# A recurrent-memory attention kernel whose streamed weights are loaded in halves, later, in a new order

## The chip, the cores and the metric

The kernel runs on one core of a Trainium2 chip. The metric is the device time of one execution in microseconds. Before the change three runs took 3192.28, 3196.55 and 3191.59 us (median 3192.28).

TensorE appears as PE for the matmuls and as PEld for the weight loads that overlap them; VectorE is DVE, ScalarE is ACT, GpSimd is POOL, and SyncE is SP, which here does nothing but issue DMAs.

## The reference

The input is 2048 tokens of width 640. It goes through two layers with the same weights; each layer has a part A and a part B, and each part is added to its input.

```python
# A: 64 segments of 32 tokens, one after the other, with a memory of 8 rows
for s in range(n_seg):
    h = concatenate([mem, x[s*32:(s+1)*32]])          # 40 rows of 640
    q, k, v = h @ Wq, h @ Wk, h @ Wv                  # 32 heads of 192
    p = softmax(where(mask, q @ k.T * 192**-0.5, -1e9))
    o = (p @ v) @ Wo                                  # 40 rows of 640
    mem = o[:8]; out[s] = o[8:]                       # the memory goes on
# B: on all tokens
h  = gelu(layernorm(x) @ w1)                          # 640 x 640
hs = shift_four_groups(h) @ w2                        # 640 x 640, by 1 or 2 tokens
x1 = x + hs
y  = x1 + gelu(layernorm(x1) @ w3) @ w4               # 640 x 1536 x 640
```

The memory makes part A sequential: segment s+1 needs the first 8 output rows of segment s. All of Wq, Wk, Wv (640 x 6144 each) and Wo are used in every segment.

## The kernel before, in words

The two layers run as two lanes, the second five segments behind the first, so that most of the 69 steps (`T_A`) work on one segment of each lane at once: 2 x 40 = 80 rows. A step of attention walks over four pairs of head groups (`NPAIR`; a group has 4 heads, so 768 columns of a weight, `GW`; a pair has 1536, `PW`). Odd steps walk the pairs backwards, so that the last pair of one step is the first of the next and its weights are kept. For each pair there are projections for keys and queries (L1743: the weight is the stationary operand, the 80 rows stream), values (L1790, L1817, L1848: the rows are stationary), and for each of its two groups scores (L1868), a softmax on DVE and ACT (L1880, L1887, L1891 to L1893), transposes (L1903), the product with the values (L1920) and the output projection (L1946). Between them lies part B of the segments that are through, in chunks of two steps (L2142 to L2476).

The weights do not all fit in SBUF. Of the five row blocks of 128 of a weight, a part stays in resident tiles (`wk`, `wq`, `wv`, `wo`, made once by `res_tile`), and `STREAM` says how many blocks of each pair are read again in every step: 4, 2, 2, 4 for keys and queries, 3, 1, 1, 4 for values. `load_pair` (L1587) streams each such block as one DMA of 128 rows x 1536 columns (384 KB) into a ring of 12 buffers (`RING_A`, tile name `wst`). One such block serves both groups of the pair, so its buffer comes free only after the second group's projections. Weights of part B go through a ring of 3 buffers (`load_b`, `wstB`). All of these DMAs stand in one queue, SP's, in order.

In which order each engine's instructions stand is decided ahead of time by `Plan.place`, which is a list scheduler with costs of its own: operations of an engine are sorted by a rank (the table `RANK`, else the due time), and placed when their operands are ready by its estimate. For SP it also waits until its estimate of the DMA backlog is under `DMA_AHEAD` us; such a DMA is called paced, and is given a wait on the matmul that should end just before it (`PACE`). In the first and last steps at most `FLYING` of SP's weight DMAs may be under way. SP's DMAs also take turns on eight completion semaphores, so that each waits until the eighth before it has landed. PE's order is fixed by this plan; the hardware then runs the queues as they stand, each waiting on semaphores.

For the last chunk of part B there is no step left that could cover its loads. `homes` lists places inside resident tiles of the last two pairs that are no longer needed; 13 of its 19 loads go there, and the other six into the streaming ring.

Of the kernel before, what the change touches and what calls it, by code (L numbers as in the profile page):

```python
# [11 lines left out]
bf16 = mybir.dt.bfloat16  # L12
# [10 lines left out]
RING_A = 12  # L23
# [33 lines left out]
DMA_ISSUE = 0.37  # L57
# [5 lines left out]
DMA_AHEAD = 1.0  # L63
DMA_AHEAD_ONE = 1.0
DMA_START = 375.0e3
RATE_ONE = 350.0e3
NSTEPS = 64
LAST_PACE = 0.55
FLYING = 5
# [9 lines left out]
        "apply_ln.f": (626742377, 1381540087, 2899948923, 3305595292,),  # L79
        "chunk.f1": (-45861084,),  # L80
        "chunk.f2": (-45659757,),
        "chunk.f3": (1142445880,),
        "chunk.fe": (681528837,),
        "chunk.fe3": (3558561887,),
        "chunk.fel": (929138305,),
        "chunk.fhr": (1690223076,),
        "chunk.fhs": (3263874326,),
        "chunk.fk0": (585175460,),
        "chunk.fk1": (2899747596,),
        "chunk.fs": (3237320380, 3237521706,),  # L90
        "chunk.ft": (256864035,),
        "chunk.ftl": (1386157383,),
        "chunk.fw": (1690089438, 1635248815, 1663407949, 3135586750, 2850300232, 2661990109, 3573417949,
            3572573150, 3675059769, 3969648649, 3957741830, 4039975132, 4549482156,),
        "chunk.fx": (257065362,),
        "chunk.fx0": (1526572645, 1386869158,),
        "chunk.fxu": (3348674608,),
        "gelu.f1": (1699890861, 1945196059, 3675261096, 3920708539, 4184197392, 4484921572, 4620347075,),
        "gelu.f2": (1699825810, 2028698272, 3681545875, 3947181960, 4202989764, 4549896008, 4584775502,),
        "gelu.f3": (1700027137, 2490379395, 3745281954, 3957725317, 4362469546, 4620334608, 4623504062,),  # L100
        "gelu.f4": (1944994732, 2631326347, 3850812073, 3948320419, 4362670872, 4550298661, 4623468787,),
        "ln_ops.f1": (429292543, 3237723033,),
        "ln_ops.f2": (585056509, 3305393966,),
        "load_b.fn": (-910488622, -944871371, -932829747, 2409305095, 2322445750, 2257234409, 2921458646,
            2661468021, 3186012878, 3602555507, 3601991726, 3600713583, 4110587825,),
        "transposes.f": (681327511, 3546956339,),
    },
    "chunk_0": {
        "apply_ln.f": (-9435854, 1110510770, 1460067902,),
        "chunk.f1": (-416043209635,),  # L110
        "chunk.f2": (-282216187950,),
        "chunk.f3": (166275964,),
        "chunk.fe": (-11203768,),
        "chunk.fe3": (1569789630,),
        "chunk.fel": (316814938,),
        "chunk.fhr": (608520262,),
        "chunk.fhs": (1149152527,),
        "chunk.fk0": (773149199,),
        "chunk.fs": (1129996849, 1129996849,),
        "chunk.ft": (-171210997,),  # L120
        "chunk.ftl": (166477291,),
        "chunk.fw": (574133776, 547786658, 574316317, 1085014019, 1105500739, 1129795522, 1570217486,
            1570328582, 1492728232, 3006190713, 3006190784, 3006714875, 3168347961,),
        "chunk.fx": (-84446892,),
        "chunk.fx0": (515277332, 361838522,),
        "chunk.fxu": (1578287371,),
# [8 lines left out]
        "transposes.f": (-54228973, 1485017325,),  # L135
    },
    "chunk_1": {
        "apply_ln.f": (56483562, 141981145, 1588087148, 1857952252,),
        "chunk.f1": (-5799992,),
        "chunk.f2": (69525817,),  # L140
        "chunk.f3": (141963611,),
# [1228 lines left out]
def kernel(  # L1370
# [16 lines left out]
    nc = tc.nc  # L1387
    P = 128
# [6 lines left out]
    KC = Dm // P  # L1395
# [1191 lines left out]
```

## Time and profile before

| what | value |
|---|---|
| median of three runs | 3192.28 us |
| the profiled execution, time | 3207.95 us |
| the profiled execution, span | 3206.2 us, 158605 instructions |
| PE busy | 3098.9 us, 97% |
| PEld, DVE, ACT, POOL busy | 86%, 64%, 54%, 16% |
| moved by DMA | 859.45 MB, mean 268 GB/s |
| SP's queue (q1) | 796.08 MB, 75.6% of the 16 engines' time |

PE's busy time says where PE had a matmul under way. What is left, some 107 us, are gaps, and each has something that ended it: a DMA that landed, a result of DVE or ACT, or "issue", where no semaphore was being waited for. The first 100 us hold the largest part of it, since nothing is in SBUF yet. The queue of DMAs is the second thing to look at: q1 carries the weights, q8 the instructions themselves in blocks of 16 KB, q0 the transfers that POOL issues.

### The profile page before, as it was taken

The numbers are of one execution on the slowest core, as the hardware profiler recorded it, in microseconds if no ns is written. First come the engines' busy times: TensorE is split into PE (matmuls) and PEld (weight loads), VectorE is DVE, ScalarE is ACT, GpSimd is POOL, SyncE is SP. The second block draws the span as 40 slices with busy tenths as digits, with TensorE's granted clock in tenths as the row PEclk, the third lists the DMA queues.
The fourth block names the chain that finished last, engine by engine and source line by source line (L and its number), as shares of the span: only waits on it lengthen the run. The fifth ranks groups of instructions, "written<-read, shape, count | busy, mean of one in ns | idle before, by whom it ended". The sixth has DMA issues, their size and how long they took to land.

```text
span 3206.2 us, 158605 instructions
## 1 busy us (share of the span) xinstructions
PE 3098.9 (97%) x70198; PEld 2765.0 (86%) x70201; DVE 2053.9 (64%) x6448; ACT 1720.1 (54%) x3985; POOL 497.6 (16%) x983
## 2 busy tenths in 40 slices
PE   5899999999999999999999999999999999999997
PEld 4778888988988989888889888888898889888876
DVE  3566566666666666666666666666666666666665
ACT  1335555555555555565555555555565565556443
POOL 1001111111111111111111111111111111110000
PEclk7999999999999999999999999999999999999999
DMA  9888788878888888888788888888888888888786
GB/s 378 275 262 260 252 281 267 259 247 275 267 263 266 288 256 266 261 279 268 252 274 278 257 258 261 276 257 260 289 264 256 260 276 269 260 267 284 256 283 213
DMA packets 421673, 859.45 MB, mean 268 GB/s; under 512 B 48334, under 2 KB 216223, under 8 KB 420984
## 3 DMA queue, kind: packets, MB, share of 16 engines
q1 hardware_dynamic: 396776, 796.08, 75.6%
q0 software_dynamic: 24032, 53.12, 5.5%
q8 instruction: 550, 9.01, 1.2%
q14 instruction: 139, 1.14, 0.1%
q10 hardware_dynamic: 176, 0.09, 0.0%
HBM read 823.73 MB, written 25.37 MB: 265 GB/s over the span
## 4 chain that ended last, share of the span: by engine, by line
PE 90%; DMA 6%; issue 2%; DVE 1%; ACT 1%; POOL 0%; SPq 0%; POOLq 0%; DVEq 0%; ACTq 0%
PE psk L1743 17%; PE psy L1946 17%; PE psq L1743 17%; PE psv L1790 12%; PE pso L1920 5%; PE pss L1868 4%; PE psv L1817 3%; PE y L2422 3%; PE psh L2376 3%; PE pst L1903 2%; PE psv L1848 2%; DMA wst<-in_A_Wq_dram 1%; PE hs L2313 1%; PE psh L2253 1%; DMA wst<-in_A_Wk_dram 1%
## 5 line engine op out<-in xcount | busy, mean ns | idle before, releaser
L1743 PEld LDWEIGHTS <-wst 128*128 128x128 bf16 x19872 | 826.7, 99 | 88.6 <-issue 39.4
L1946 PE MATMUL psy<-oT,wo 128*128 128x80 bf16 (+1 forms) x16560 | 712.1, 200 | 13.5 <-issue 7.0
L1946 PEld LDWEIGHTS <-wo 128*128 128x128 bf16 x16560 | 639.2, 99 | 54.9 <-issue 30.7
L1778 ACT CAST V<-psv 32x384 bf16<-32x384 f32 (+3 forms) x1032 | 487.5, 473 | 363.1 <-PE psv L1790 276.2
L1743 PE MATMUL psq<-hT,wst 128*128 128x80 bf16 (+1 forms) x9936 | 558.3, 200 | 10.8 <-DMA wst<-in_A_Wq_dram 7.0
L1743 PE MATMUL psk<-hT,wst 128*128 128x80 bf16 (+1 forms) x9936 | 543.3, 200 | 19.5 <-issue 7.8
L1753 ACT CAST qT<-psq 128x480 bf16<-128x480 f32 (+1 forms) x552 | 292.6, 530 | 348.6 <-PE psq L1743 277.1
L1880 DVE CUSTOM_DVE_ANT_1 pss<-pss,mask 80x320 f32<-80x320 f32 (+2 forms) x552 | 257.1, 466 | 296.8 <-ACT V L1778 145.4
L1768 DVE CAST kT<-psk 64x160 bf16<-64x160 f32 (+1 forms) x1104 | 339.6, 308 | 161.5 <-PE psk L1743 78.2
L1928 ACT CAST oT<-pso 128x480 bf16<-128x480 f32 (+1 forms) x552 | 292.6, 530 | 242.7 <-PE pso L1920 224.5
L1887 ACT ACTIVATE Pm<-pss,sm 80x320 bf16<-80x320 f32 (+2 forms) x552 | 278.5, 505 | 185.5 <-DVE sm L1880 90.3
L1743 PE MATMUL psk<-hT,wk 128*128 128x80 bf16 (+1 forms) x6624 | 321.4, 200 | 10.1 <-DMA wk<-in_A_Wk_dram 6.4
L1743 PE MATMUL psq<-hT,wq 128*128 128x80 bf16 (+1 forms) x6624 | 321.0, 200 | 2.5 <-issue 0.9
L1891 DVE TENSOR_REDUCE sm<-Pm 80x4 f32<-80x320 bf16 (+2 forms) x552 | 249.5, 452 | 102.7 <-ACT Pm L1887 96.1
L1761 DVE CAST kT<-psk 128x320 bf16<-128x320 f32 (+1 forms) x552 | 253.3, 459 | 75.8 <-PE psk L1743 66.3
L1790 PEld LDWEIGHTS <-hT 128*128 128x128 bf16 x2320 | 203.8, 98 | 98.9 <-issue 0.7
L1798 POOL DMA_DIRECT2D vahead<-V x232 | 119.8, 516 | 1071.0 <-ACT V L1778 1037.1
L1790 PE MATMUL psv<-wv,hT 128*128 128x384 bf16 x1276 | 284.1, 326 | 0.0
L1893 DVE TENSOR_TENSOR Pm<-Pm,sm 80x320 bf16<-80x320 bf16 (+2 forms) x552 | 255.7, 463 | 42.4 <-DVE sm L1892 0.5
L1743 PEld LDWEIGHTS <-wk 128*128 128x128 bf16 x6624 | 267.8, 100 | 12.8 <-DMA wk<-in_A_Wk_dram 6.6
L1743 PEld LDWEIGHTS <-wq 128*128 128x128 bf16 x6624 | 270.4, 100 | 7.6 <-issue 4.8
L1911 ACT COPY PT<-pst 80x320 bf16<-80x320 bf16 (+2 forms) x552 | 219.9, 398 | 104.9 <-PE pst L1903 93.5
(136 smaller groups left out, 4119.1 us busy)
## 6 DMA issues: line engine op xcount, KB each, us to landing
wst<-in_A_Wk_dram SPq DMA_DIRECT2D x556, 384.0 KB, 4.9
wst<-in_A_Wq_dram SPq DMA_DIRECT2D x556, 384.0 KB, 4.9
wstB<-in_B_w_dram SPq DMA_DIRECT2D x495, 320.0 KB, 4.5
wst<-in_A_Wv_dram SPq DMA_DIRECT2D x383, 384.0 KB, 4.9
wstB<-in_B_w_dram SPq DMA_DIRECT2D x132, 160.0 KB, 4.0
vahead<-V POOLq DMA_DIRECT2D x232, 84.0 KB, 3.9
V<-vahead POOLq DMA_DIRECT2D x232, 84.0 KB, 4.7
wo<-in_A_Wo_dram SPq DMA_DIRECT2D x8, 960.0 KB, 10.9
```

The lines of the kernel that those rows point to most:

```text
L1743: nc.tensor.matmul(out=o[:, cc, 0:W], lhsT=wv(kc, GW * j + cc * P, GW * j + (cc + 1) * P), rhs=h[:, kc, cw:cw + W], start=begin(pq), stop= ...
L1753: nc.scalar.copy(out=qT[G % QT_BUFS][:, :, c0:c0 + N], in_=T(pq)[:, :, off:off + N])
L1761: nc.vector.tensor_copy(out=k4[:, :, 0::3, c0:c0 + N], in_=p4[:, :, 0::2, off:off + N])
L1768: copy(out=k4[r0:r1, :, jj, c0:c0 + N], in_=p4[r0:r1, :, 1, off:off + N])
L1778: (nc.vector.tensor_copy if e == "DVE" else nc.scalar.copy)(out=v_part(*dst), in_=a_)
L1790: nc.tensor.matmul(out=T(bank)[:], lhsT=left[:, kc, :], rhs=wv(kc, GWH * b, GWH * (b + 1)), start=(kc == 0), stop=(kc == KC - 1))
L1880: nc.vector.tensor_tensor_reduce(out=o, in0=o, in1=maskt.unsqueeze(1).to_broadcast([NR, HG, N]), scale=-scale, scalar=3.0e38, op0=ALU.add, ...
L1887: nc.scalar.activation(out=Pb[0:NR, :, 0:N], in_=o, func=ACT.Exp, bias=sm_[0:NR, 0:1], scale=-1.0)
L1891: nc.vector.tensor_reduce(out=sm_[0:NR, 2:2 + HG], in_=Pb[0:NR, :, 0:N], axis=AX.X, op=ALU.add)
L1893: nc.vector.tensor_tensor(out=Pb[0:NR, :, 0:N], in0=Pb[0:NR, :, 0:N], in1=sm_[0:NR, 6:6 + HG].unsqueeze(2).to_broadcast([NR, HG, N]), op=A ...
L1928: nc.scalar.copy(out=o_[:, :, off:off + N], in_=T(pso)[:, :, 0:N])
L1946: nc.tensor.matmul(out=o[:, m, cw:cw + W], lhsT=wo[:, cc, m * P:(m + 1) * P], rhs=o_[:, cc, 0:W], start=st, stop=True, skip_group_check=True)
```

## The change

Each streamed block is now loaded as two DMAs, one for each head group: 128 rows x 768 columns, 192 KB, into a ring of 24 buffers of half the size. The ring has the same bytes. A matmul of the first group waits only for the first half and frees it without the second. The pacing limit goes from 1.0 to 0.85 us of estimated backlog, the limit on flying DMAs from 5 to 9, and the estimated rate in the first and last steps from 350 to 345 GB/s. All loads of the last chunk go into resident tiles, since they no longer fit a buffer of the ring; for this the list of homes takes in the first two pairs, but for one tile that holds other data. The table of ranks is replaced, so that the order on every engine is new. The computation and the shapes of all matmuls are the same.

```diff
-RING_A = 12
+RING_A = 24
-DMA_AHEAD = 1.0
+DMA_AHEAD = 0.85
-RATE_ONE = 350.0e3
+RATE_ONE = 345.0e3
-FLYING = 5
+FLYING = 9
 RANK = {
...
-    SLOT = PW
+    SLOT = GW
...
-        for j, kc in enumerate(range(nres, KC)):
+        for u, (kc, j) in enumerate((kc, j) for kc in range(nres, KC) for j in range(2)):
             b = Slotted("ra", None)
             b.make = lambda b=b: wring.tile([P, SLOT], bf16, name="wst", tag=f"ra{b.slot}")
-            def fn(op, b=b, kc=kc):
-                nc.sync.dma_start(out=T(b)[:, 0:PW], in_=w_src[kind][:, kc, cols])
-            add("SP", DMA_ISSUE, due - now + 0.01 * j, fn, w=(b,), dma=2 * P * PW, queue="wa")
+            def fn(op, b=b, kc=kc, c0=PW * pr + GW * j):
+                nc.sync.dma_start(out=T(b)[:], in_=w_src[kind][:, kc, c0:c0 + GW])
+            add("SP", DMA_ISSUE, due - now + 0.005 * u, fn, w=(b,), dma=2 * P * GW, queue="wa")
             slots.append(b)
         def view(kc, c0, c1):
             if kc < nres:
                 return rt[:, kc, c0:c1]
-            return T(slots[kc - nres])[:, c0:c1]
+            j = c0 // GW
+            return T(slots[2 * (kc - nres) + j])[:, c0 - GW * j:c1 - GW * j]
         return (rb, *slots), view
-    homes = [(k, pr, u) for pr in range(NPAIR - 2, NPAIR) for k in "kqv"
+    homes = [(k, pr, u) for pr in range(NPAIR) for k in "kqv" if (k, pr) != ("v", 1)
              for u in range((KC - STREAM[k][pr]) * PW // (2 * Dm))]
     def load_b(nm, a, e, due, c0=0, c1=None, last=False):
-        if last and homes:
+        if last:
...
         else:
-            b = Slotted("ra" if last else "rb", None)
+            b = Slotted("rb", None)
...
-                    wb = wbs[0] if kcs[0] == 0 else wbs[1 + kcs[0] - nres]
+                    wb = wbs[0] if kcs[0] == 0 else wbs[1 + 2 * (kcs[0] - nres) + j]
```

## The prediction

> **What bounds the kernel now.** I read the page's first two parts, then the busy time by stage, then what PE waited for, then the DMA queue.
>
> ```profile
> span 3206.2 us, 158605 instructions
> PE 3098.9 (97%) x70198; PEld 2765.0 (86%) x70201; DVE 2053.9 (64%) x6448; ACT 1720.1 (54%) x3985; POOL 497.6 (16%) x983
> ...
> q1 hardware_dynamic: 396776, 796.08, 75.6%
> ...
> wst<-in_A_Wk_dram SPq DMA_DIRECT2D x556, 384.0 KB, 4.9
> ...
> wstB<-in_B_w_dram SPq DMA_DIRECT2D x132, 160.0 KB, 4.0
> ```
>
> PE is the bound. How much of it is left to gain differs by stage (columns: stretch, PE, PEld, DVE, ACT, POOL busy, granted clock, DMA share, GB/s):
>
> ```profile
> 0.00:100.00 100.00, 61.42 (x1264) 50.75 (x1265) 31.17 (x115) 19.60 (x56) 9.01 (x33) 0.81 0.98 356
> 100.00:200.00 100.00, 91.08 (x2508) 77.93 (x2504) 59.50 (x228) 39.89 (x122) 2.27 (x5) 0.97 0.82 277
> 1300.00:1400.00 100.00, 99.75 (x2218) 90.06 (x2217) 67.38 (x205) 56.63 (x127) 17.73 (x35) 1.00 0.84 270
> 3000.00:3100.00 100.00, 93.04 (x2476) 79.54 (x2473) 68.43 (x242) 43.59 (x125) 7.50 (x15) 1.00 0.83 279
> ```
>
> The first 100 us are bound by DMA (share 0.98), the middle by PE, and there the DMA engines are already five sixths busy. From 300 to 2900 us PE's gaps come to only 26 us in 2600; the first 300 us hold 53, the end from 2900 on 24. What ended them (total, times, longest):
>
> ```profile
> PE psk L1743 <- issue: 11.5, 10, 2.8
> PE psk L1743 <- ACT hT L2484: 7.2, 28, 0.3
> PE psq L1743 <- DMA wst<-in_A_Wq_dram: 7.0, 9, 2.4
> PE psy L1946 <- issue: 7.0, 9, 2.1
> PE psy L1946 <- DMA wo<-in_A_Wo_dram: 2.9, 3, 2.0
> ```
>
> Over all lines "issue" ended 28.6 us. The 28 such gaps over 0.3 us stand at every 256th instruction of PE or a multiple of that (place 193 or 194 modulo 256), 2.2 to 3.3 us after a 16 KB packet of q8 started: PE waits for its own instructions. DMAs of `wst` ended 10 us, 3.3 of it in 300 to 2900 us and 1.7 later.
>
> **The change, part by part.** The sum is made against the profiled execution, 3207.95 us (span 3206.2 and 1.75 around it); the median of the runs, 3192.28, lies 15.7 below it, and I carry the same change over.
>
> *More packets.* 1495 streamed DMAs become 2990. The trace's packets of 3072 B take 121 ns (median), those of 1280 B 55, those of 4 B (the completion marks, 16 per DMA) 9. A line through the first two gives 64.5 ns for 1536 B, so a row costs 129 instead of 121. Over the run that is 1495 x 128 x 8 ns / 16 = 96 us of all engines, and 1495 x 9 ns = 13 for marks: 3.4% of the span. The middle's DMA share goes from 0.83 to some 0.865; still not the bound. Where DMA is the bound it shows: PE's last large wait at the start is for `wo`, at 86 us, and 33 whole transfers stand in SP's queue up to that load in both orders (31.6 MB in both). 33 x (128 x 8 / 16 + 9) ns = 2.4 us later. Bounds: 0 if two halves cost what a whole one does; +7 if the engines starve, since eight semaphores let only eight halves (1.57 MB) be under way: at the 4.9 us of the page's landing that is 321 GB/s against the 388 of 10 to 80 us, 40.4 us instead of 33.5 for the 13.0 MB. I take +3, since eight halves are 4.2 us of packets and the quickest landings of the trace took 3.2.
>
> *Issued later, with finer waits.* I counted, in the two instruction orders, the matmul work between the matmul that a streamed DMA waits for (its own wait or that of one ahead of it in the queue) and the first matmul that needs it, with the trace's start-to-start intervals (36 ns at 80 columns, 56 at 128, 136 at 320, 163 at 384). In the middle the shortest hundredth of these leads is 5.36 us before and 4.88 after, the shortest twentieth 5.87 and 5.13. Landings spread too: of those of `wst` in the middle a tenth took over 5.58 us. A half spends 0.52 us in the engines, a whole transfer 0.97, so its landing should be 0.45 shorter: 4.45 in the median (the 160 KB row says 4.0) and 5.13 at the ninth tenth. Before, that tenth stays 0.29 under the shortest twentieth of leads; after, it meets it. Leads with less than half a microsecond over the median landing: 17 of 1239 (under 5.4) before, 45 of 2480 (under 4.94) after; with less than 0.9, 48 and some 200. Lateness in the middle and at the end cost 5.0 us before; at 2.6 times the thin leads it is 13. Value +8. Bounds: -5 if halves land in 4.0 (nothing is late then), and +25 if they land like whole ones (of the whole run's leads after the start 298 are under 5.4, 85 us short in sum, of which I let a quarter to a third come to bear, since a late wait moves the ones behind it).
>
> The 1022 further waits on DMAs in PE's stream cost nothing: 899 matmul starts of L1743 with one wait have the same median interval, 36 ns, as those without. SP issues 1495 more DMAs at 0.33 to 0.38 us, 0.5 ms in all; SP waits for PE for 1.9 ms, and that is the cover. What a late issue would hold up is the queue behind it, `wstB` and `wo` included. POOL's queue has the same transfers.
>
> *Instructions of PE.* They come over the same engines. A packet of q8 behind a transfer that has just been issued waits up to 0.97 us before and 0.52 after, but there are twice as many, and more load. Bounds: every one of the 28 gaps loses 0.45 us (-13), and the clock stays up: the trace's clock shows five windows of 3.41 us at half speed after 150 us, each some 10 us behind a gap of 1.7 us or more, 1.7 us each, of which four could go (-7), -20 in all; or the fuller engines add as much as a seventh (+4). I take -4, nearer the second, because the leads above show that the queue is paced by PE and not by its own length. The Trainium skill, Runtime: NRT & Kernel Launch, section Instruction fetch mechanics, says that crossing a 16 KiB boundary is mostly hidden; with that the term would be 0 and the sum 4 us higher. The 28.6 us of this trace speak against it.
>
> *New order.* In the middle the pattern repeats every two steps (91.4 us), and a bubble of 0.4 us there costs 28 x 0.4 = 11. The shortest work between a matmul and the matmul that needs its result through ACT or DVE decides. Scores to transposes: 3.12 before, 2.99 after (the shortest twentieth), for a chain L1880, L1887, L1891, L1893 of 0.47 + 0.51 + 0.45 + 0.46 = 1.89 us; L1920 to L1946 1.08 in both for a copy of 0.53; L1743 to L1868 0.93 in both. The one bubble there, psn to hT to L1743 (7.2 us), has no work in between in either order and stays. So 0; bounds -7 (it goes) and +11 (a new one). At the start, where the first lane is alone, the new order is tighter: scores to transposes 1.79 before and 1.04 after against those 1.89, the least between L1903 and L1920 0.63 and 0.28, between L1743 and L1868 0.80 and 0.14. Gaps that DVE or ACT ended came to some 19 us there without the first wait of 10; I take +3, bounds -4 and +8. The first matmul may come 3 us sooner, since x is now first in the queue; that gains nothing, because the bytes up to `wo` end the stage.
>
> *Last chunk.* Its loads are issued 5.4 us or more ahead of their use (4.0 before), the cover being the chain of the last chunk through DVE and ACT; without it, half a microsecond. The limit of 9 never acts, since the semaphores stop at eight; 0.
>
> Sum: +3 + 8 - 4 + 0 + 3 + 0 = +10 us: 3218 for a profiled execution, **3202** for the median.
>
> **The rivals.**
>
> *A: shorter queues let instructions and weights through (faster).* For it: "issue" is the largest single cause of gaps, and backlog is what both edits of the pacing lower. With 12 of the 20 us above, and with the 5 us of lateness gone, less 3 for packets: -14, 3178. It decides when halves land in 4.2 us or less. Against it: the leads were cut by as much as the landings.
>
> *B: halves land like whole transfers (much slower).* The wait in front of PE's matmuls is then +25 and the start +7: with the rest, some +30, 3222. For it: landings of 160 KB are only 0.9 us under those of 384 KB, and the engines are fuller. The Trainium skill, DMA: Bandwidth & Descriptors, section Bandwidth, wants at least 1 MiB per DMA for 75% of the peak, because most of a small transfer is a fixed cost; its fit of 2.0 us plus bytes at 436 GB/s gives, as an estimate, 2.45 us for a half and 2.90 for a whole one. By its rule the change loses; by the trace whole transfers followed each other every 0.98 us at the start, so the fixed part is overlapped.
>
> *C: it evens out (same).* More thin leads, each with less to lose, and a slightly lighter start: within 6 us of 3192. That the limit of 9 does nothing is certain; that half transfers do not relieve the ring is likely, as the leads show.
>
> **How the numbers follow.** The forecast (slower by some 10, between 3196 and 3214) has 0.45, B 0.12, C 0.20, A 0.23. Repeated runs of this kernel tell 0.2%, 6.4 us, from no change. Of the forecast's case a sixth (0.07) falls within 0.2%, so slower is 0.50, same 0.27, faster 0.23. The range goes from A's 3174 to B's 3224, leaving out a tenth on each side.
>
> **What would show it.** Right: gaps of PE ended by `wst` rise from 10 to some 18 us, `wst` lands in some 4.4 us, 3072 B packets become 1536 B ones of about 64 ns, PE's last wait for `wo` stands near 89 us, "issue" stays over 20 us, and DMA share in the middle is near 0.865. Wrong: "issue" halved and landings of 4.2 or less (A); landings near 4.9 with many waits of L1743 on `wst` (B); or a gap that comes back every 91 us, which would put the order, not the DMA, at fault.

## The result, and the profile after

The changed kernel took 3223.9 us in the median of five runs (3223.55 to 3229.33), the kernel before 3193.97 us beside it (3191.59 to 3196.55): a ratio of 1.0099, with a 95% interval of 1.0084 to 1.0114. By the ratio that is 32 us more (30 by the two medians), where 10 were forecast. The profiled execution after took 3227.25 us.

The execution that the prediction was worked from (span 3206.2 us) was a long one of its kind: a second profile of the unchanged kernel has a span of 3188.4 us. Both stand in the tables below, since two executions of one kernel differ by 18 us here, and a comparison of two single profiles can be off by as much. The ratios come from several runs on one chip each.

The first parts of the page of the changed kernel:

```profile
span 3225.5 us, 161658 instructions
PE 3106.5 (96%) x70199; PEld 2765.5 (86%) x70201; DVE 2052.9 (64%) x6448; ACT 1723.4 (53%) x3985; POOL 497.3 (15%) x983
...
q1 hardware_dynamic: 612056, 796.18, 77.5%
...
PE 80%; DMA 14%; issue 2%; DVE 1%; ACT 1%; POOL 0%; SPq 0%; POOLq 0%; ACTq 0%; DVEq 0%
```

The same bytes go through q1 in 612056 packets instead of 396776, and the last line, the chain that ended last, gives DMA 14%; it was 6% and 4% in the two profiles of before. The same stretches as in the prediction (columns: stretch, PE, PEld, DVE, ACT, POOL busy, granted clock, DMA share, GB/s):

```profile
0.00:100.00 100.00, 59.31 (x1206) 47.92 (x1206) 30.22 (x112) 18.59 (x52) 8.97 (x33) 0.78 0.99 345
100.00:200.00 100.00, 89.73 (x2419) 74.66 (x2420) 58.43 (x218) 39.45 (x120) 2.26 (x5) 0.98 0.83 268
1300.00:1400.00 100.00, 99.14 (x2164) 88.62 (x2161) 63.92 (x197) 56.69 (x128) 16.47 (x32) 1.00 0.85 271
3000.00:3100.00 100.00, 89.93 (x2379) 76.88 (x2375) 65.61 (x239) 42.55 (x122) 7.81 (x16) 0.98 0.85 274
```

PE is busy for less of each of these stretches, most clearly at the start and the end, where it was 61.42 and 93.04 before. What it waited for (total, times, longest):

```profile
PE psk L1789 <- DMA wst<-in_A_Wk_dram: 23.3, 33, 5.1
PE psq L1789 <- DMA wst<-in_A_Wq_dram: 21.3, 29, 4.5
...
PE psk L1789 <- ACT hT L2530: 7.4, 29, 0.3
PE psk L1789 <- issue: 4.4, 4, 1.4
```

L1789 is the L1743 of before. "issue" led the list of this line with 11.5 us; now it is 4.4, and the two rows for `wst` lead instead. Their landings (from the view of DMA issues, the last number in us):

```profile
wst<-in_A_Wq_dram SPq DMA_DIRECT2D x1112, 192.0 KB, 4.6
wst<-in_A_Wk_dram SPq DMA_DIRECT2D x1112, 192.0 KB, 4.5
```

Before, the page gave 4.9 for both, the second profile 4.8:

```profile
wst<-in_A_Wk_dram SPq DMA_DIRECT2D x556, 384.0 KB, 4.8
```

Half the bytes land 0.2 to 0.4 us sooner, no more. Summed over all of PE's lines, by stage (the first step, steps 1 to 5, steps 6 to 61, the rest; a step ends with its last matmul of the output projection; gaps over 0.05 us, where the lists above have those over 0.15):

| kernel | stages, us | gaps ended by `wst` | by issue |
|---|---|---|---|
| before, first profile | 87.2, 211.6, 2586.4, 321.1 | 4.6, 0.5, 3.3, 1.7 | 0, 8.5, 9.9, 10.2 |
| before, second profile | 87.7, 207.2, 2576.4, 317.1 | 4.8, 0.3, 1.1, 0.1 | 0, 7.6, 7.4, 11.0 |
| after | 90.9, 214.3, 2593.7, 326.7 | 16.4, 6.7, 14.8, 9.0 | 0, 3.9, 1.2, 4.2 |

So two things happened that work against each other: late instructions went from 26 to 29 us down to 9, and late weights from 6 to 10 us up to 47. In the first step `wst` only takes the place of other waits (gaps of 40 us in the first 100 us in the second profile of before and in that of after); behind it, 30.5 us stand against 1.5 to 5.5.

These sums do not reach the 30 us yet, because a gap is not the whole cost of a wait. PE's busy time grew too, with the same matmuls; the second profile of before has

```profile
span 3188.4 us, 158605 instructions
PE 3086.5 (97%) x70198; PEld 2758.9 (87%) x70201; DVE 2053.5 (64%) x6448; ACT 1717.6 (54%) x3985; POOL 496.3 (16%) x983
```

against 3106.5 after. The record of a matmul of 80 columns lasts 202 ns in the mean, and the next one usually starts 36 ns after it: the first 0.17 us of a wait count as busy. Counted from start to start, over the usual distance, the waits that `wst` ended behind the first step came to 53 us, 10 and 3 in the two profiles of before; waits for PE's instructions (those that show as gaps) came to 11 us, 37 and 33 before. So late weights cost 44 to 50 us and late instructions gave back 21 to 26. With 3 to 4 us in the first step and 6 to 7 of waits for other loads, `wstB` among them, this adds up to 27 and 39 us, where the spans differ by 19 and 37.

### The profile page after: what moved, and what is told of

It is laid out like the page before. It is cut to its first block, busy times and chain, and to the rows that moved or that the text cites. A ratio compares the mean times of both kernels' runs of the same rounds, so it can differ in the third digit from the quotient of the medians.

```text
span 3225.5 us, 161658 instructions
## 1 busy us (share of the span) xinstructions
PE 3106.5 (96%) x70199; PEld 2765.5 (86%) x70201; DVE 2052.9 (64%) x6448; ACT 1723.4 (53%) x3985; POOL 497.3 (15%) x983
## 3 DMA queue, kind: packets, MB, share of 16 engines
q1 hardware_dynamic: 612056, 796.18, 77.5%
## 4 chain that ended last, share of the span: by engine, by line
PE 80%; DMA 14%; issue 2%; DVE 1%; ACT 1%; POOL 0%; SPq 0%; POOLq 0%; ACTq 0%; DVEq 0%
PE psy L1992 16%; PE psk L1789 15%; PE psq L1789 15%; PE psv L1836 11%; DMA wst<-in_A_Wk_dram 6%; PE pso L1966 4%; PE pss L1914 4%; DMA wst<-in_A_Wq_dram 4%; PE psh L2422 3%; PE psv L1863 3%; PE y L2468 3%; PE pst L1949 2%; PE hs L2359 1%; PE psv L1894 1%; DMA wst<-in_A_Wv_dram 1%
## 5 line engine op out<-in xcount | busy, mean ns | idle before, releaser
L1789 PEld LDWEIGHTS <-wst 128*128 128x128 bf16 x19872 | 822.0, 99 | 127.8 <-DMA wst<-in_A_Wk_dram 31.7
L1992 PE MATMUL psy<-oT,wo 128*128 128x80 bf16 (+1 forms) x16560 | 695.9, 200 | 3.2 <-issue 1.0
L1992 PEld LDWEIGHTS <-wo 128*128 128x128 bf16 x16560 | 628.8, 99 | 27.6 <-issue 13.8
L1789 PE MATMUL psk<-hT,wst 128*128 128x80 bf16 (+1 forms) x9936 | 568.1, 200 | 37.2 <-DMA wst<-in_A_Wk_dram 23.3
L1824 ACT CAST V<-psv 128x384 bf16<-128x384 f32 (+4 forms) x1032 | 485.8, 474 | 199.1 <-PE psv L1863 75.5
L1789 PE MATMUL psq<-hT,wst 128*128 128x80 bf16 (+1 forms) x9936 | 550.0, 200 | 26.0 <-DMA wst<-in_A_Wq_dram 21.3
L1789 PE MATMUL psk<-hT,wk 128*128 128x80 bf16 (+1 forms) x6624 | 320.7, 200 | 2.0 <-issue 1.3
L1789 PE MATMUL psq<-hT,wq 128*128 128x80 bf16 (+1 forms) x6624 | 320.0, 200 | 2.5 <-DMA wq<-in_A_Wq_dram 1.8
L1789 PEld LDWEIGHTS <-wk 128*128 128x128 bf16 x6624 | 272.1, 100 | 7.2 <-issue 3.3
L1789 PEld LDWEIGHTS <-wq 128*128 128x128 bf16 x6624 | 266.0, 99 | 4.1 <-DMA wq<-in_A_Wq_dram 1.9
## 6 DMA issues: line engine op xcount, KB each, us to landing
wo<-in_A_Wo_dram SPq DMA_DIRECT2D x8, 960.0 KB, 10.2
```

The source lines that it names most:

```text
L1789: nc.tensor.matmul(out=o[:, cc, 0:W], lhsT=wv(kc, GW * j + cc * P, GW * j + (cc + 1) * P), rhs=h[:, kc, cw:cw + W], start=begin(pq), stop= ...
L1824: (nc.vector.tensor_copy if e == "DVE" else nc.scalar.copy)(out=v_part(*dst), in_=a_)
L1992: nc.tensor.matmul(out=o[:, m, cw:cw + W], lhsT=wo[:, cc, m * P:(m + 1) * P], rhs=o_[:, cc, 0:W], start=st, stop=True, skip_group_check=True)
```

## Experiments

The theory at the start: thin leads. A streamed half is issued too late for its landing, because the new order and the smaller `DMA_AHEAD` cut the lead and the half size does not shorten the landing. The rivals: the half size itself costs (packets, or number of DMAs), or the new order costs by waits between engines.

### One part of the change at a time

The kernel before once more, unchanged:

> The kernel before, unchanged, for a second profile, since its profiled execution (3207.95 us) lies 14 us above the median of its other runs (3193.97). If that was one disturbed execution, this profile comes at 3190 to 3200 with fewer gaps that 'issue' ended than 28.6 us; if the profile of this kernel is always slower, it comes near 3208 again.

Half transfers with the old ranks, each rank of a streamed load given to both halves, and the old pacing:

```diff
 # the changed kernel, but
-DMA_AHEAD = 0.85
+DMA_AHEAD = 1.0
-RATE_ONE = 345.0e3
+RATE_ONE = 350.0e3
-FLYING = 9
+FLYING = 10
 RANK = {   # the table of the kernel before; for the streamed loads:
-    "load_pair.fn": (r0, r1, ...)
+    "load_pair.fn": (r0, r0, r1, r1, ...)
```

> Halves alone: the changed kernel's half transfers and ring of 24, with the ranks, the pacing limit of 1.0 and the rate of 350 of the kernel before; each half has the rank that the whole transfer had, so both stand together in SP's queue. Theory 'halves cost' (packets, marks, landings that shrink less than the work per transfer): 3210 to 3224. Theory 'order costs' and theory 'later issue costs': 3190 to 3200, since leads stay those of before and landings can only get shorter.

Whole transfers (ring of 12) with the new ranks, the first half's rank for each, and the new constants:

```diff
 # the kernel before, but
-DMA_AHEAD = 1.0
+DMA_AHEAD = 0.85
-RATE_ONE = 350.0e3
+RATE_ONE = 345.0e3
 RANK = {   # the table of the changed kernel; for the streamed loads:
-    "load_pair.fn": (r0, r1, r2, r3, ...)
+    "load_pair.fn": (r0, r2, ...)
```

> The order alone: whole transfers and the ring of 12, with the new ranks (each whole transfer at its first half's rank), the pacing limit of 0.85 and the rate of 345. Theory 'halves cost': 3190 to 3202. Theories 'order costs' and 'later issue costs': 3212 or more; whole transfers need 0.45 us more of the shorter lead, so even over 3224.

The changed kernel with one constant back:

```diff
-DMA_AHEAD = 0.85
+DMA_AHEAD = 1.0
```

> The changed kernel with its pacing limit of estimated backlog back at 1.0 us, so that streamed DMAs are issued some 0.15 us of backlog earlier; the ranks are the new ones. Theory 'later issue costs': at least 10 of the 30 us come back, 3214 or less, and gaps of PE ended by streamed weights in 300 to 2900 us fall from 14.8 to under 8 us. Theories 'halves cost' and 'order costs': 3219 to 3228.

Measured, as ratios to the kernel before: unchanged 0.9994 (0.9984 to 1.0004); half transfers in the old order 1.0032 (1.0017 to 1.0047), median 3204.9 us; whole transfers in the new order 1.0555 (1.0528 to 1.0582), 3372.0 us; the changed kernel with 1.0 1.0080 (1.0058 to 1.0102), 3221.4 us. The halves lie between the ranges of both theories. The changed kernel with 1.0 missed what 'later issue costs' asked for, 3214 us and under 8 us of gaps in the middle: these came to 10.0, and its interval overlaps that of the changed kernel.

In whole transfers with the new order PE's waits on streamed weights are most of the story, 146 us of gaps over the run (same columns as above; the table of ranks takes fewer lines there, so L1743 is L1288):

```profile
PE psk L1288 <- DMA wst<-in_A_Wk_dram: 81.4, 78, 5.1
PE psq L1288 <- DMA wst<-in_A_Wq_dram: 58.3, 44, 5.6
```

The new order leaves whole blocks 2.64 us in the shortest hundredth of leads, so it stands or falls with the halves. The halves alone cost a third of the loss (10 us); the other two thirds come from the order and its pacing.

Where the halves in the old order lose is seen at the start. In four profiles of theirs (this one, two with another `DMA_AHEAD`, one with the new end) the first step took 92.4 to 96.2 us; in six of whole blocks with the old order (before, twice, and its versions with another `DMA_AHEAD` or `FLYING`) it took 87.0 to 87.7. Behind the first step this kernel's profile, 3106 us, lies between the two of before, 3119 and 3101.

### Is it the size of the packets or the number of the DMAs?

A whole block in one DMA, its buffer with 8 unused columns behind each half, so that each row becomes two packets of 1536 B:

```diff
 # the kernel before, but
-    SLOT = PW
+    GP = GW + 8
+    SLOT = 2 * GP
...
-                nc.sync.dma_start(out=T(b)[:, 0:PW], in_=w_src[kind][:, kc, cols])
+                nc.sync.dma_start(out=T(b)[:].rearrange("p (g n) -> p g n", g=2)[:, :, 0:GW],
+                                  in_=w_src[kind][:, kc, cols].rearrange("p (g n) -> p g n", g=2))
...
-            return T(slots[kc - nres])[:, c0:c1]
+            j = c0 // GW
+            return T(slots[kc - nres])[:, GP * j + c0 - GW * j:GP * j + c1 - GW * j]
```

> The kernel before, with each streamed block still one DMA of 384 KB into one of 12 buffers, but its buffer has 8 unused columns between the two halves, so that every row is two packets of 1536 B instead of one of 3072 B. Order, waits and number of DMAs are the kernel's before. Theory S (the packets' own time): 8 ns more per row of a block, so the first 100 us, where the DMA engines are full, get 2 us longer, the middle's DMA share rises by 0.025, and the time is 3194 to 3198. Theory N (what the halves lose at the start, some 9 us, is packets of half the size altogether): the start loses 7 us or more, 3200 to 3206. If the half transfers' loss at the start is their number (completion, eight in flight), then this run loses nothing there: 3191 to 3195.

The same with quarters of a row, 768 B each (`GW // 2` for `GW`, `g=4`, and 4 unused columns):

> The kernel before, each streamed block still one DMA of 384 KB, its rows now in four packets of 768 B (two of 1536 B gave ratio 1.0040, 1.0025 to 1.0056). Theory S (the packets' own time, by which whole transfers land later: 4.75 to 5.02 us in the median with 1536 B): a row takes some 145 ns for 121 and 129, three times the addition, so landings of 5.5 us or more and a ratio of 1.009 to 1.016; the middle's gaps ended by wst rise to 10 us or more. Theory Z (the 0.4% of the run before was something else, such as the place of the buffers in SBUF): ratio 1.003 to 1.005 again.

Two DMAs of 64 rows with whole rows, into the same buffer:

```diff
 # the kernel before, but
-                nc.sync.dma_start(out=T(b)[:, 0:PW], in_=w_src[kind][:, kc, cols])
+                nc.sync.dma_start(out=T(b)[0:64, 0:PW], in_=w_src[kind][0:64, kc, cols])
+                nc.sync.dma_start(out=T(b)[64:P, 0:PW], in_=w_src[kind][64:P, kc, cols])
...
+        lead = nc.cur_bb.bb.instructions[k]
...
-                tc.add_manual_dep(o.last, flying[-1 - FLYING].last.name, dep, reason="flying")
+                tc.add_manual_dep(lead, flying[-1 - FLYING].last.name, dep, reason="flying")
...
-                tc.add_manual_dep(o.last, done[k].last.name, dep, reason="pace")
+                tc.add_manual_dep(lead, done[k].last.name, dep, reason="pace")
```

> The kernel before, each streamed block as two DMAs of 64 rows with whole rows of 3072 B into the same buffer; order and pacing are the kernel's before, the first of the two has the waits. So there are as many DMAs of 192 KB as with half transfers, but no smaller packets, and a matmul still waits for the whole block. In all runs with half transfers issue ended 9 to 16 us of PE's gaps for 26 to 29 before, and in the runs with smaller packets alone it did not fall (28, and 50 with 768 B). Theory S (the packet size is the loss, the number of DMAs is none): ratio 0.998 to 1.001, gaps ended by issue 18 us or less. Rival N (the number of DMAs, with their completions and semaphores, is the loss): ratio 1.002 to 1.005.

Packets of 1536 B gave 1.0040 (1.0025 to 1.0056), packets of 768 B 1.0202 (1.0184 to 1.0220): 13 and 64 us. Theory N fell: the first step took 89.6 us, 2 more, not 7, so of the 5 to 9 us that halves lose there most is not the packets' size. Theory S was exceeded as well (3207 us by the ratio, for 3194 to 3198), and where the 13 us lie is not shown, since the profiled execution with 1536 B, 3202.02 us, was 10 us shorter than the median. The packets' medians are 121, 65 and 36 ns, so a row costs 121, 130 and 144 ns, and whole blocks land in 4.75, 5.02 and 5.45 us (medians of the middle). With 768 B, the queue (packets, MB, share of 16 engines) and the landing of a block, from the view of DMA issues:

```profile
q1 hardware_dynamic: 970856, 796.08, 82.1%
...
wst<-in_A_Wk_dram SPq DMA_DIRECT2D x556, 384.0 KB, 5.6
```

The same kernel's stretch of the middle, with the columns given above:

```profile
1300.00:1400.00 100.00, 98.57 (x2184) 88.73 (x2183) 65.17 (x201) 56.37 (x128) 16.34 (x32) 1.00 0.91 267
```

That is 0.7 us more per block than before (4.9). The GB/s hardly move (270 before), the DMA share does (0.84 before): the engines take longer for the same bytes. And that is paid by PE, in the middle, with a DMA share that stays under 1: steps 6 to 61 took 2627.2 us, 2586.4 and 2576.4 before (waits from 300 to 2900 us, 768 B):

```profile
PE psq L1748 <- issue: 10.1, 10, 1.8
PE psy L1951 <- issue: 7.4, 12, 1.9
...
PE psh L2258 <- issue: 4.9, 3, 2.3
PE psq L1748 <- DMA wst<-in_A_Wq_dram: 4.1, 11, 0.8
```

Issue over the run is 50.2 us with 768 B, 28.2 with 1536 B, 26.0 and 28.6 before, and 12.8 with half transfers in the old order. So it does not follow the packets; in these four kernels it rises with the time that one DMA holds an engine: 8 rows and a mark are 8 x 121 + 9 ns = 0.98 us before, 8 x 130 + 9 = 1.05 with 1536 B, 8 x 144 + 9 = 1.16 with 768 B, and 8 x 65 + 9 = 0.53 for a half. The Trainium skill, DMA: Bandwidth & Descriptors, section Queues, rings and completion order, says that an engine drains a packet of typically 9 to 17 descriptors from one queue before it turns to the next. These four numbers agree with it, if the instructions' queue waits for what one DMA put on an engine; but the trace does not show the turns themselves, and the next run and the longer queue (below) do not follow from it.

Two DMAs of 64 rows were no clean test, because they are another transfer: 1.2137 (1.2094 to 1.2180). Their landing, from the view of DMA issues:

```profile
wst<-in_A_Wk_dram SPq DMA_DIRECT2D x1112, 192.0 KB, 6.6
```

And their stretch of the middle:

```profile
1300.00:1400.00 100.00, 86.64 (x1766) 75.44 (x1766) 51.27 (x157) 43.05 (x97) 14.54 (x28) 0.95 0.87 211
```

A landing takes 1.7 us longer than before for half the bytes, and PE has lost an eighth of the stretch, at 211 GB/s for 270. A packet of 3072 B took 206 ns in the median there, for 121. Issue came to 144 us, the most of all runs, though one DMA should hold an engine for 4 x 206 + 13 ns = 0.84 us here, if its 64 rows are spread evenly (an estimate; there are 16 marks per DMA as before). So that time alone does not set issue. Over all twenty profiles it goes with the landing of `wst` in the middle: issue in steps 6 to 61 is 0.7 to 5.4 us where the median landing is under 4.6 us, 2.7 to 10.5 from 4.75 to 5.02, 39.9 at 5.37, 32.1 at 5.45 and 128.6 at 6.88. Instructions are late where every transfer is late; which causes which is not shown.

What the number of DMAs costs by itself stays open. The half transfers' 0.32% and the packets' 0.40% differ by less than their intervals, and the halves' part holds a gain in issue that the packets' does not.

### Pacing

`DMA_AHEAD` alone was changed, in three kernels: whole transfers in the old order with 0.85 and 2.0, half transfers in the old order with 0.85 and 2.0, and the changed kernel with 2.0.

```diff
 # the kernel before / the halves in the old order
-DMA_AHEAD = 1.0
+DMA_AHEAD = 0.85    # or 2.0
 # the changed kernel
-DMA_AHEAD = 0.85
+DMA_AHEAD = 2.0
```

> The kernel before with DMA_AHEAD 0.85 for 1.0, nothing else. Leads in the middle under 5.8 us go from 48 to 85 of 1239, under 5.4 from 17 to 19. With half transfers in the old order the same edit cost 0.15 hundredths of the time at most. Theory L (it is the leads that count, and they hardly change): ratio 0.999 to 1.002. Theory P (the later issue is a loss in any order): 1.002 to 1.005.

> The kernel before with DMA_AHEAD 2.0 for 1.0, nothing else: leads in the middle under 5.8 us 29 for 48, the shortest twentieth 6.76 us for 5.87. Theory L: wst ends under 1 us of gaps in the middle (1.1 and 3.3 in two profiled executions before), ratio 0.998 to 1.000. Theory Q (a longer queue holds back PE's instructions, and issue is the largest cause here): issue in the middle rises from 7 to 10 us to 14 or more, ratio 1.001 to 1.004.

> Half transfers with the old order and DMA_AHEAD 0.85 for 1.0, nothing else. Leads in the middle under 5.8 us go from 28 to 117 of 2480, under 5.4 from 6 to 7. Theory L: the later issue alone costs 2 to 6 us with the old order, ratio 1.004 to 1.005. Theory P (0.85 is what is too late, in any order): ratio 1.006 to 1.008, with gaps ended by wst in the middle of 10 us or more. The remainder to the run with the old order in the middle alone (1.0071) is then what the new start and end cost.

> Half transfers in a ring of 24 with the old order, and DMA_AHEAD 2.0 for 1.0. Against the same with 1.0 (3204.9 us) the leads in the middle grow from 5.58 to 6.60 us at the shortest hundredth. Theory L: gaps ended by wst in the middle go from 2.7 us to under 1, the time is 3199 to 3205, since start and end keep theirs. Theory Q (a longer queue holds back PE's instructions): issue in the middle rises from 5.4 to 8 us or more and the time is 3205 to 3212.

> The changed kernel with DMA_AHEAD 2.0 for 0.85, nothing else. Leads of streamed weights in the middle: shortest hundredth 6.02 us for 4.88, under 5.4 us 6 for 237. Theory L (thin leads): gaps ended by wst in the middle fall from 14.8 us to 2 or less, the middle's loss of 17 us goes by 12 or more, the time is 3207 to 3213 (the start and the end keep their 10 us each). Theory O (the new order loses in the middle by its chains through ACT and DVE): the middle keeps 8 us or more of its loss, 3215 to 3222. Theory Q (a longer queue holds back PE's instructions): gaps ended by issue rise from 9.2 us to 18 or more over the run and take back most of it, 3216 to 3224.

Measured: whole with 0.85 1.0012 (0.9999 to 1.0025), whole with 2.0 1.0106 (1.0078 to 1.0133); halves in the old order with 0.85 1.0047 (1.0030 to 1.0063), with 2.0 1.0031 (1.0018 to 1.0044); the changed kernel with 2.0 1.0075 (1.0063 to 1.0087).

The largest surprise is the whole blocks with the longer queue (waits from 300 to 2900 us):

```profile
PE psq L1743 <- issue: 9.4, 10, 1.6
PE psy L1946 <- issue: 8.7, 11, 1.7
PE psk L1743 <- issue: 7.9, 14, 1.4
PE psv L1817 <- issue: 7.5, 7, 1.6
```

Steps 6 to 61 have 39.9 us of issue there, 7.4 to 9.9 before: theory Q, at a ratio far above its 1.001 to 1.004. With half transfers the same 2.0 leaves it at 2.7. That halves let PE's instructions through, and whole blocks in a long queue do not, is shown; why the queue's length matters for the one and not for the other is not.

The table puts the middle of each kernel together. The lead is counted in the instruction orders as in the prediction (shortest hundredth); landings are those of `wst` between 300 and 2900 us (median, ninth tenth, 99th hundredth), as far as the trace has them (six to eight tenths of the DMAs); the last two columns are gaps of PE.

| kernel | lead, 1% | landing 50, 90, 99% | lead less landing 99% | `wst`, steps 6 to 61 | issue, all |
|---|---|---|---|---|---|
| halves, old order, 2.0 | 6.60 | 4.81, 5.64, 6.41 | +0.19 | 0.3 | 10.2 |
| halves, old order, 0.85 | 5.58 | 4.42, 5.24, 5.98 | -0.40 | 0.7 | 5.4 |
| halves, old order, 1.0 | 5.58 | 4.55, 5.43, 6.08 | -0.50 | 2.5 | 12.8 |
| after, with 2.0 | 6.02 | 4.88, 5.80, 6.83 | -0.81 | 7.8 | 14.1 |
| after, with 1.0 | 5.16 | 4.52, 5.41, 6.17 | -1.01 | 10.0 | 7.9 |
| after | 4.88 | 4.54, 5.51, 6.34 | -1.46 | 14.8 | 9.3 |
| before, second profile | 5.36 | 4.75, 5.64, 6.20 | -0.84 | 1.1 | 26.0 |
| before, first profile | 5.36 | 4.83, 5.58, 6.52 | -1.16 | 3.3 | 28.6 |

In these six rows for half transfers the lateness rises as the fourth column, the distance between the two tails, falls, while the medians of the landings give no such order. Of two kernels below, the halves with the new start fit (-0.70 and 5.9 us), the changed kernel with the old middle does not (-0.71 and 11.4); both have a joint that may have a part in it. Whole blocks lose less at the same distance, there being half as many. The change took 0.48 us off the lead and left the landing's tail where it was, 6.34 us between 6.20 and 6.52.

The lead ends its count at the matmul that releases a DMA, and SP may issue it later. Matching the instruction orders to the traces shows how much later (from the release to SP's issue, streamed blocks from 300 to 2900 us), and how often SP waited there until an earlier DMA had landed:

| kernel | issue after release, 50, 90, 99% | shortest hundredth from issue to use | SP's waits for a landing |
|---|---|---|---|
| before, both profiles | 0.07, 0.11, 0.34 | 5.45, 5.35 | 30, 31 |
| after | 0.11, 0.77, 1.40 | 4.49 | 161 |
| after, with 2.0 | 0.79, 2.06, 3.03 | 4.81 | 475 |
| halves, old order, 1.0 | 0.11, 0.73, 1.41 | 5.22 | 203 |
| halves, old order, 2.0 | 0.75, 1.99, 3.14 | 5.50 | 420 |

Halves leave late as whole blocks do not: there are twice as many to issue, at 0.33 to 0.38 us each, and each waits for the eighth before it. The change took not 0.48 us but 0.9 off the shortest time from issue to use, and 2.0 gave back not 1.14 us but 0.3. With these times the rows above do not keep their order (5.50 less 6.41 goes with 0.3 us of `wst`, 5.22 less 6.08 with 2.5), but the new order still stands about half a microsecond or more under the old. The tails say which kernel is late, not by how much.

Theory L is right that the thin leads make the weights late, and its number for 2.0 was wrong: 7.8 us of `wst` for 2 or less, and 1.0075, some 3218 us, for 3207 to 3213. Nor did the middle of that profile get shorter, 2593.2 us for 2593.7: issue there went from 1.2 to 7.3 us and the waits for other loads from 3.6 to 5.3. By its time the run would fit theories O and Q too. Against O stand the gaps that other engines ended in the middle, 11.6 us for 10.2; against Q, issue of 14.1 us over the run for 18 or more.

### Order

The changed kernel with the old ranks in the middle (`step0`, `step1`, `chunk`, `chunk_end`), and the halves in the old order with the new ranks in the start or in the end alone:

```diff
 RANK = {   # of the changed kernel, but with these four tables from the kernel before
     "chunk": {...}, "chunk_end": {...}, "step0": {...}, "step1": {...},
 # the halves in the old order, but with these tables from the changed kernel
     "start", "first", "second", "head2" to "head6", "chunk_0" to "chunk_2", "chunk_end_0" to "chunk_end_2"
 # or these
     all "tail", "last" and "end" tables
```

> The changed kernel with the old ranks in the middle (the tags step0, step1, chunk and chunk_end, each rank of a streamed load given to both halves); halves, ring, DMA_AHEAD 0.85, start and end stay as changed. The changed kernel loses 17 us in the middle against the kernel before, and streamed weights (wst) end 14.8 us of PE's gaps there. Theory L (thin leads: the new order and the later issue together leave streamed weights too little time): in the instruction orders, leads under 5.4 us in the middle fall from 237 of 2480 to 15, so gaps ended by wst in the middle fall from 14.8 to 3 us or less, the middle comes out within 4 us of the kernel before, and the time is 3205 to 3211. Theory P (0.85 us of backlog is too late in any order): little changes, 3218 to 3224. Theory H (half transfers themselves fill the engines): 3218 to 3224 as well, with wst still ending over 10 us in the middle.

> Half transfers with the old order (3204.9 us, ratio 1.0032 to the kernel before), but with the new ranks in the start (the tags start, first, second, head and the first three chunks); the middle, the end and the pacing stay old. The changed kernel and the one with the old order in the middle alone both wait 15 to 16 us for wst in their first 100 us, where the old order waits for 4. Theory E (the new order at start and end costs some 11 us of the 27 beyond the packets): about half of it is here, ratio 1.004 to 1.006, with gaps ended by wst of over 12 us in the first 100 us. Theory M (it is the middle and its pacing alone): ratio 1.002 to 1.004, since what the start loses to wst it gains on DVE.

> Half transfers with the old order, but with the new ranks in the end (all tail tags, end and last). Theory E: ratio 1.004 to 1.006, with gaps ended by wst after 2900 us of 8 us or more (5.6 with the old order, 9.0 in the changed kernel). Theory M: ratio 1.002 to 1.004, gaps after 2900 us unchanged at some 23 us.

Measured: the changed kernel with the old middle 1.0071 (1.0055 to 1.0087), a miss of theory L; the halves with the new start 1.0057 (1.0041 to 1.0073), with the new end 1.0045 (1.0032 to 1.0058).

The first two are dearer than their parts, for a reason of their own (the new start as theory E had it, the new end at the edge between E and M): where the new start meets the old middle there are waits that neither kernel has (the halves with the new start, 300 to 480 us):

```profile
PE pso L1465 <- ACT PT L1456: 1.5, 1, 1.5
PE psk L1288 <- DMA wst<-in_A_Wk_dram: 1.2, 2, 0.9
PE psh L1921 <- DVE h2u L1602: 1.0, 1, 1.0
```

Steps 7 to 10 take 187.6 and 186.2 us in these two, 182.0 and 180.6 before and 180.9 in the changed kernel. With those 6 us taken off (an estimate from single profiles), the new start costs nothing that these runs can tell, and the changed kernel with the old middle stands at some 1.005: the new order of the middle then accounts for some 0.5%, 15 us, with 0.85 as its pacing; without that correction it is 0.28%, 9 us. The new end is 4 us by the ratios, whose intervals overlap; its stage took 330.1 us for 321.5, with 9.1 us of `wst` for 5.7.

### How many may fly

The limit on flying DMAs was put back in the changed kernel, and shortened in the kernel before:

```diff
 # the changed kernel
-FLYING = 9
+FLYING = 5
 # the kernel before
-FLYING = 5
+FLYING = 4    # or 3
```

> The changed kernel with FLYING 5 for 9, as before the change; the order is the same. In the prediction the limit of 9 was costed at nothing, since eight completion semaphores stop the queue first. Five halves in a landing of 4.5 us are 218 GB/s. If the limit matters only where it stops the queue, 5 makes the first and last steps slower: ratio 1.012 to 1.020 for 1.010, with gaps ended by wst outside the middle up from 32 us to 45 or more. Rival Q (a shorter queue lets instructions and weights through): 1.005 to 1.009.

> The kernel before with FLYING 4 for 5: in the first and last steps at most four of SP's weight DMAs are under way; the order is the same. With a longer queue in the middle (DMA_AHEAD 2.0) issue grew from 7 to 38 us; at start and end issue ends 19 us of gaps and wst under 2. Theory Q (the queue's length sets how late PE's instructions come): issue outside the middle falls from 19 to 15 us or less and the ratio is 0.997 to 0.999, unless weights come late. Theory T (four under way are too few): gaps ended by weights outside the middle and the first 100 us rise by 4 us or more, ratio 1.000 to 1.003.

> The kernel before with FLYING 3 for 5. Three transfers of 384 KB in a landing of 4.9 us are 241 GB/s. Theory Q and T together: issue outside the middle at 12 us or less, but weights late by 20 us or more in the first and last steps, ratio 1.003 to 1.010.

Measured: 1.0198 (1.0179 to 1.0216) for the changed kernel with 5; 1.0021 (1.0010 to 1.0032) and 1.0137 (1.0114 to 1.0160) for 4 and 3 before, the last above its range. In the changed kernel with 5 the waits are (whole run):

```profile
PE psq L1789 <- DMA wst<-in_A_Wq_dram: 35.3, 37, 4.5
PE psk L1789 <- DMA wst<-in_A_Wk_dram: 27.8, 43, 4.0
```

With 4 whole blocks issue falls from 26.0 to 15.4 us and `wst` rises from 6.3 to 21.7: a shorter queue does let instructions through, and pays more for it in weights. No kernel tried was faster than the one before.

## Why the prediction was wrong

The direction was right, by the mechanism named; the size was a third of what came. That 3223.9 us lies where rival B was put (3222) is in part luck: B had 25 us for late weights and 4 off for instructions, the runs have 44 to 50 and 21 to 26. By its steps:

- **More packets, +3, in the middle nothing.** The packet's time was right (64.5 ns forecast, 65 measured), and the first step is 3 to 4 us longer in this one profile (5 to 9 with halves in the old order, near the +7 that was the bound for eight under way). The cover was wrong. "Still not the bound" does not mean free: packets of 1536 B alone cost 13 us (8 to 18), outside the bounds of 0 to 7, and those of 768 B, a row of which takes 23 ns more rather than 9, 64 us.
- **Issued later, with finer waits, +8. This is the step that failed.** Gaps ended by `wst` behind the first step rose by 25 to 29 us, where +25 was the upper bound and rival B's value. The leads up to the release were counted rightly. What failed first was to take 0.45 us off the whole distribution of landings because a half spends 0.45 us less in the engines. The median lost 0.2 to 0.3 us, the ninth tenth 0.1 (5.51 for 5.58 and 5.64, and 5.13 were forecast). In the middle a half was issued with six of SP's DMAs under way in the median and then landed after 4.7 us, while one that found none landed after 2.4; a whole block was issued with three under way and landed after 4.8 (landings that the trace lacks were taken as 4.5 us). Six halves are as many bytes as three whole blocks, so the part of a landing that is spent behind others did not shrink. Rival B's premise, halves that land like whole blocks, was nearly true where it matters. I gave it 0.12.
- **The same step, SP as cover.** That SP waits for PE for 1.9 ms was taken as cover for 1495 more issues. A tenth of the halves left over 0.77 us after their release, 0.11 before, so the shortest leads lost 0.9 us and not 0.48. And the price was taken from gaps, each of which leaves out some 0.17 us of its wait.
- **Instructions of PE, -4.** The gain was 17 to 19 us in gaps, more than the -13 that was the bound without the clock. The reason given against it, that PE paces the queue, did not carry: the ten kernels with half transfers have 1.4 to 14.1 us of issue, 26 to 29 before. Rival A's mechanism was there in full, and was paid for with weights. The windows of half clock begin within 1.1 us of the end of their gaps, not some 10 us behind, and within the run those after 150 us are five and one in the two profiles of before and three after: the clock gained nothing. What the prediction quoted from the Trainium skill (Runtime: NRT & Kernel Launch, section Instruction fetch mechanics), that a crossing is mostly hidden, holds by count: of the 550 blocks of 256 that PE runs, 28 and 26 show a gap over 0.3 us before and 8 after. By time the rest is not nothing, 26 to 29 us before and 60 with the longer queue.
- **New order.** In the middle 0 was right for waits between engines (gaps ended by DVE, ACT, PE and POOL: 10.2 us, 9.8 and 10.2 before). At the start the +3 came out as no bubbles (4.5 us in steps 1 to 5, 5.8 and 6.2 before) but late weights, 6.7 us. The order's cost lies where I had booked it under leads.
- **Last chunk, 0.** Gaps ended by engines in the last stage are 12.6 us, 13.0 and 13.3 before. The limit of 9 never acts, as said; that 5 would have cost 1% shows that halves need more.

One reading of the view is off without touching the sum: the 24 us of gaps from 2900 us on end at 3200; the last 6 us hold 4.6 more. And the fit quoted under rival B stands in another section of that page of the Trainium skill, Anatomy of one DMA, and is for DMAs that GpSimd issues, where SP issues these.

From the ratios, the 32 us are some 10 for the halves in the old order, some 5 for 0.85 in place of 1.0 (0.15%, which its intervals do not separate from nothing) and 17 for the new order, most of it in the middle and the end. Of the first 10, the first step shows 5 to 9. The rest of the halves' 0.3% could not be read from a stage: the three executions with old ranks throughout that were profiled have middles of 2569 to 2577 us, no longer than before, while those kernels' medians lie 1 to 16 us above the profiled times. That eight under way are too few at the start is argued from the bytes and from 358 to 370 GB/s between 10 and 80 us, 389 before; no run had more than eight.

## What to carry to other kernels

When a transfer is cut in two, compare the short tail of the leads, counted from the issue and not from the release, with the long tail of the landings, and let the landing be that of the queue it stands in: the part spent in the engines shrinks, the time behind the others does not. Price a wait from start to start, since a gap leaves out the part that the last matmul covers. A DMA share of 0.84 was no cover for smaller packets here: with 768 B PE's own instructions came late by 22 to 24 us more, so look at the gaps at every 256th instruction before costing packets at nothing. And a table of ranks is tuned to its transfers: the new one cost 5.6% with whole blocks, and pieces of two tables joined cost some 6 us at the joint alone, so a part tried by itself is not the part in its place.

## What was not expected of the hardware

DMAs into 64 of the 128 rows were much slower per byte than those into all: 206 ns for a packet of 3072 B, for 121, and 246 GB/s for 389 between 10 and 80 us. The Trainium skill, DMA: Bandwidth & Descriptors, section The descriptor swizzle, has rows 0 to 63 behind one half of the ports into SBUF and rows 64 to 127 behind the other; the slower packets agree with that, and no run here shows the ports themselves.

Letting SP's queue grow from 1 to 2 us of estimated backlog, with nothing else changed and the leads longer (shortest twentieth 6.76 us for 5.87), cost 34 us, with PE's instructions late (issue 60.3 us for 26.0).
